# Retention attention ahead of two MLPs: the chunk of 256 tokens worked in two pieces of 128

## The chip, the cores and the metric

One core of one Trainium2 chip runs the whole program in one launch. The metric is the device time of that launch in microseconds (us); lower is better. Of a kernel's runs the median counts.

## The reference

```python
def _attn_ref(q, k, v):                       # (4, 8, 768, 64), float32
    gamma = 1.0 - 2.0 ** (-5.0 - np.arange(H))
    scale = 1.0 / np.sqrt(D)
    for t in range(S):
        state = gamma * state + np.einsum('bhd,bhe->bhde', k[:, :, t], v[:, :, t])
        y[:, :, t] = scale * np.einsum('bhd,bhde->bhe', q[:, :, t], state)

def reference(...):
    x = attn_out.transpose(0, 2, 1, 3).reshape(3072, 512)
    h = x @ w_in;  x = np.maximum(0.01 * h, h) @ w_out          # d_ff 2048
    h = np.maximum(x @ w2_in, 0.0);  return h * h @ w2_out
```

A state of 64x64 per batch and head decays by gamma with each token and takes up one outer product of key and value; each token's output is its query times the state. The result goes through two MLPs.

## The kernel before, in words

The sequence of 768 tokens is cut into NC = 3 chunks of C = 256 tokens, of which each has 4 batches and 4 pairs of heads, so 16 *pairs* per chunk and 48 in all (the list `ups`, lines 120 and 121). Two heads of 64 dimensions share the 128 partitions. Within a chunk the attention is done as matrix products, between chunks a state is carried:

- `load_pair` (line 127) fetches a pair's queries, keys, values and keys again in another layout. In the first chunk a pair is one tile of 512 KB with eight buffers; later a pair has two tiles `r`.
- `prep_pair` (line 142) makes, on VectorE (DVE), `qs` = queries times the decay since the chunk's start (chunks 2 and 3) and `vs` = values times the decay to its end (chunks 1 and 2).
- `scores` (line 159) makes on TensorE (PE) keys times queries for both heads into two PSUM banks `sc`: the second 128 keys against the second 128 queries (128 columns), the first 128 keys against all 256 queries (256 columns). DVE multiplies the three blocks of 128 columns by the mask with the decay into `pm` (line 176).
- `values` (line 180) sums in one PSUM bank `y` (its pool has one buffer) `state` times `qs` (chunks 2 and 3), then the values times `pm`. ScalarE (ACT) copies `y` to `xs` (line 200), the input of the MLP. Then `sp` = keys times `vs`, a matmul of 128x128 in another bank, of which the two diagonal blocks go into the state: by ACT in the first chunk (line 211), by DVE in the second (line 213).

float32 matmuls run as two passes each, so PE's records are twice the matmuls. The matmuls of the two heads use different halves of the array and run side by side.

`mm` (line 111), `load` and `store` pin the order of PE, of SyncE's DMA queue (SP) and of GpSimd's (POOL) to the order of the code. DVE and ACT are ordered by a scheduler as the program is built, and each then runs strictly in that order. `attend` (line 240) does the scores of pair n+1 and then the values of pair n.

The first chunk's 16 pairs run almost alone on PE at the start of the program, two pieces of the first MLP (`emit_plain`) standing among the last pairs. Meanwhile ACT and DVE convert the first weights: `cast` (line 271) takes `sg` as loaded, two operations on ACT (lines 275, 276), three on DVE (277, 278, 281); `pair_up` (line 300) splits the result into two halves, one copy on ACT (301) and one subtraction on DVE (302); `split` (line 56 of that part, 417 and 418 of the file) does the same with `xs`, giving `xh` and `xl`. The pairs of the chunks 2 and 3 are strewn into the first MLP's blocks b = 0 and 1: eight each through `score_next` and `value_to` in the loop over q (lines 826 to 859), eight each through `attend` in the loop over i (line 893).

Of the kernel before, what the change touches and what calls it, by code (L numbers as in the profile page):

```python
# [9 lines left out]
F32 = mybir.dt.float32  # L10
# [4 lines left out]
ALU = mybir.AluOpType  # L15

B, H, S, D = 4, 8, 768, 64
P = 128
C = 256
NC = S // C  # L20
NU = B * NC
NP = H // 2
# [3 lines left out]
T = 512  # L26
# [6 lines left out]
WARM = 10  # L33
# [17 lines left out]
def retention_then_two_mlps(  # L51
# [11 lines left out]
    nc = tc.nc  # L63
# [9 lines left out]
    ps_a = ctx.enter_context(tc.tile_pool(name="ps_a", bufs=1, space=bass.MemoryType.PSUM))  # L73

    early = ExitStack()
    a_p = early.enter_context(tc.tile_pool(name="a", bufs=2))
    const = early.enter_context(tc.tile_pool(name="const", bufs=1))
    late = {}

    def swap_pools():  # L80
        early.close()
        late["p"] = mid.enter_context(tc.tile_pool(name="late", bufs=1))

    def swap_left():
# [7 lines left out]
    qt = const.tile([P, NP, C], F32, name="qt")  # L92
    vt = const.tile([P, NP, 2, 2], F32, name="vt")
    mk = const.tile([P, NP, 2, 384], F32, name="mk")
    gt = const.tile([P, NP], F32, name="gt")
    state = const.tile([P, B, NP, D], F32, name="state")

# [13 lines left out]
    def mm(**kw):  # L111
        pin(nc.tensor.matmul(**kw))  # L112
# [9 lines left out]
    raw, prep, sc_ps = {}, {}, {}  # L122
    xs = {}


# [1 line left out]
    def load_pair(up):  # L127
        u, p = up
        k = u * NP + p
        n = ups.index(up)  # L130
        if u < B:
            t = g_p.tile([P, 2, T], F32, tag=f"t{n % NQ}", name="r", bufs=1)
            load(out=t.rearrange("p i c -> p (i c)"), in_=first[k])
            raw[up] = [t[:, 0], t[:, 1]]
            return
        m = T if u // B < NC - 1 else C
        t = [a_p.tile([P, T], F32, tag=f"r{i}", name="r", bufs=2 + i) for i in range(2)]
        load(out=t[0], in_=first[k, :, 0:T])
        load(out=t[1][:, :m], in_=first[k, :, T:T + m])
        raw[up] = t  # L140

    def prep_pair(up):
        u, p = up
        qk, vk = raw[up]
        qs = vs = None
        if u >= B:
            qs = a_p.tile([P, C], F32, tag="qs", name="qs", bufs=1)
            nc.vector.tensor_tensor(out=qs, in0=qk[:, 0:C], in1=qt[:, p], op=ALU.mult)
        if u < (NC - 1) * B:
            vs = a_p.tile([P, 2, 2, D], F32, tag="vs", name="vs")  # L150
            nc.vector.tensor_tensor(
                out=vs,
                in0=vk[:, 0:C].rearrange("p (b h e) -> p b h e", b=2, h=2),
                in1=vt[:, p].unsqueeze(3).to_broadcast([P, 2, 2, D]),
                op=ALU.mult,
            )
        prep[up] = (qs, vs)

    def scores(up):
        u, p = up  # L160
        qk, vk = raw[up]
        k0 = 2 * (ups.index(up) % 2)
        if u < B:
            sc = [ps_acc.tile([P, 512], F32, tag=f"acc{k0 + h}", name="sc") for h in range(2)]
        else:
            sc = [ps_h.tile([P, 512], F32, tag="h", name="sc") for h in range(2)]
        for cols, kk, qq in ((slice(128, 256), slice(P, 2 * P), slice(P, 2 * P)), (slice(256, 512), slice(0, P), slice(0, C))):
            for h in range(2):
                a = slice(64 * h, 64 * h + 64)
                mm(out=sc[h][:, cols], lhsT=qk[a, C + kk.start:C + kk.stop], rhs=qk[a, qq], start=True, stop=True)  # L170
        pm = []
        if u < B:
            both = x_p.tile([P, 2, T], F32, tag=("xh7", "xl7", "xh2", "xl2")[ups.index(up) % 4], name="pm")
        for h in range(2):
            t = both[:, h, 0:384] if u < B else a_p.tile([P, 384], F32, tag="pm", name="pm")
            nc.vector.tensor_tensor(out=t, in0=sc[h][:, 128:512], in1=mk[:, p, h], op=ALU.mult)  # L176
            pm.append(t)
        sc_ps[up] = pm

    def values(up):  # L180
        u, p = up
        c, b = divmod(u, B)
        vk = raw[up][1]
        qs, vs = prep.pop(up)
        pm = sc_ps.pop(up)
        y = ps_a.tile([P, 2, C], F32, tag="y", name="y")
        if c:
            for h in range(2):
                a = slice(64 * h, 64 * h + 64)
                mm(out=y[a, 0], lhsT=state[a, b, p], rhs=qs[a], start=True, stop=False)  # L190
        for sb in range(2):
            c0, o = (P, 0) if sb else (0, P)
            for h in (1, 0):
                mm(
                    out=y[64 * h:64 * h + 64, 0, c0:C], lhsT=vk[:, sb * P + h * D:sb * P + h * D + D],
                    rhs=pm[h][:, o:o + C - c0], start=sb == 0 and not c, stop=sb == 1,
                )
        if c not in xs:
            xs[c] = x_p.tile([P, KB, TB], F32, tag="xs", name="xs")
        nc.scalar.copy(xs[c][:, p, b * C:b * C + C], y[:, 0])  # L200
        if c < NC - 1:
            sp = ps_h.tile([P, P], F32, tag="h", name="sp")
            for sb in range(2):
                mm(
                    out=sp, lhsT=vk[:, C + sb * P:C + (sb + 1) * P], rhs=vs[:, sb].rearrange("p h e -> p (h e)"),
                    start=sb == 0, stop=sb == 1,
                )
            for h in range(2):
                a = slice(64 * h, 64 * h + 64)
                if c == 0:  # L210
                    nc.scalar.copy(state[a, b, p], sp[a, a])
                else:
                    nc.vector.scalar_tensor_tensor(
                        out=state[a, b, p], in0=state[a, b, p], scalar=gt[a, p:p + 1], in1=sp[a, a],
                        op0=ALU.mult, op1=ALU.add,
                    )
        raw.pop(up)

    n_load, n_prep, n_done = [0], [0], [0]
# [13 lines left out]

    def value_to(n):
        while n_done[0] < n:
            values(ups[n_done[0]])
            n_done[0] += 1
            loads_to(n_done[0] + 2)
# [401 lines left out]
    def second_half(b, q, pa):  # L640
# [5 lines left out]
        pb = ps_a.tile([P, 2, C], F32, tag="y", name="pb").rearrange("p h c -> p (h c)")  # L646
# [107 lines left out]

    zero = o_p.tile([P, T], F32R, tag="gh", name="zero")
    nc.vector.memset(zero.bitcast(F32), 0.0)
    idle = ps_a.tile([P, 2, C], F32, tag="y", name="idle")
    for n in range(WARM):
        nc.tensor.matmul(
            out=idle.rearrange("p h c -> p (h c)"), lhsT=zero[:, 0:P], rhs=zero, start=n == 0, stop=n == WARM - 1  # L760
        )
    nc.scalar.dma_start(out=mk[:, 0], in_=mask[:, 0])
    nc.scalar.dma_start(out=vt, in_=vtab)
    n0 = B * NP
    for p in range(1, NP):
        loads_to(2 * p)
# [10 lines left out]
        elif n in (11, 14):  # L777
            emit_plain(0, (n - 11) // 3, 0)
    split_first(1)
    nc.scalar.dma_start(out=qt, in_=qtab)  # L780
    nc.scalar.dma_start(out=gt, in_=gtab)

    def read_x(b):
        xs[NB + b] = x_p.tile([P, KB, TB], F32, tag="xs", name="xs")
# [133 lines left out]
def _tables():  # L918

    gam = (1.0 - 2.0 ** (-5.0 - np.arange(H, dtype=np.float32))).astype(np.float64)  # L920
    t = np.arange(C)
    qt = gam[:, None] ** t / np.sqrt(D)
    qtab = np.repeat(qt.reshape(NP, 2, 1, C), D, axis=2).reshape(NP, P, C).transpose(1, 0, 2)
    vt = gam[:, None] ** (C - t)
    vtab = vt.reshape(NP, 2, 2, P).transpose(3, 0, 2, 1)
    s, c = np.arange(P)[:, None], np.arange(P)[None, :]
    dec = gam[:, None, None] ** np.maximum(c - s, 0) * (c >= s)
    far = gam[:, None, None] ** (c - s + P)
    mask = np.concatenate([dec, dec, far], axis=2) / np.sqrt(D)
    mask = mask.reshape(NP, 2, P, 384).transpose(2, 0, 1, 3)  # L930
    gtab = np.repeat((gam ** C).reshape(NP, 2, 1), D, axis=2).reshape(NP, P).T
    return [np.ascontiguousarray(a, dtype=np.float32) for a in (qtab, vtab, mask, gtab)]


# [43 lines left out]
```

## Time and profile before

| what | us |
|---|---|
| three runs | 1142.53, 1143.72, 1150.15 |
| median | 1143.72 |
| the profiled execution | 1143.77 |
| its span, first to last instruction | 1141.6 |
| first matmul of the attention to the last of the first chunk | 6.0 to 54.2 |

The trace is of one execution. PE is TensorE's matmuls, PEld its weight loads, which overlap them; DVE, ACT, POOL, SP as above; a q behind a name is its queue of DMA issues. Ends of matmuls are modelled, so rows of one engine may overlap a little and the starts are what is read. Window times count from the span's start.

### The profile page before, as it was taken

To read this page: it belongs to the slowest core of one execution; us is meant where nothing else is said; L and a number is where in the kernel's file an instruction comes from. 1 tells how busy PE (TensorE), PEld (TensorE's weight loads), DVE (VectorE), ACT (ScalarE), POOL (GpSimd) and SP (SyncE) were. 2 spreads that over 40 slices of the span, in tenths; PEclk is the share of its full clock that TensorE was granted. 3 is DMA by queue.
4 is the path that set the end of the run, shared out by engine and by line. 5 is a ranking of instruction groups with operands and counts; after the bars stand their busy time and mean duration, and the time that the engine had idled before them with its cause. 6 is when DMAs were issued, how large, how long until landed. Compare 5 with 4: busy or idle time off the path is not lost.

```text
span 1141.6 us, 14068 instructions
## 1 busy us (share of the span) xinstructions
PE 1121.3 (98%) x5306; PEld 874.8 (77%) x5306; DVE 682.0 (60%) x1018; ACT 546.4 (48%) x863; POOL 74.3 (7%) x130
## 2 busy tenths in 40 slices
PE   8999999999999999999999999999999999999998
PEld 5677777767777776788888887788788888888886
DVE  5866565655443535544457567777457877555853
ACT  3745453323434333344455366665256655455542
POOL 0000000001000000000001011101011100000000
PEclk9999999999999999999999999999999999999999
DMA  9665653655555455479788878957869967257571
GB/s 373 251 236 209 221 221 121 219 178 202 194 198 203 174 190 185 157 276 345 257 320 317 316 275 327 378 212 256 294 225 359 390 211 307 83 192 247 195 241 56
DMA packets 75011, 274.35 MB, mean 240 GB/s; under 512 B 6976, under 2 KB 9024, under 8 KB 64704
## 3 DMA queue, kind: packets, MB, share of 16 engines
q1 hardware_dynamic: 57120, 197.54, 48.6%
q0 software_dynamic: 17248, 74.98, 17.2%
q8 instruction: 42, 0.69, 0.2%
q10 hardware_dynamic: 576, 0.93, 0.2%
q14 instruction: 25, 0.20, 0.1%
HBM read 197.93 MB, written 75.50 MB: 240 GB/s over the span
## 4 chain that ended last, share of the span: by engine, by line
PE 87%; DMA 7%; ACT 3%; DVE 2%; issue 1%; SPq 0%; DVEq 0%; ACTq 0%
PE acc L112 41%; PE pa L112 25%; PE pd L112 8%; PE pb L112 5%; PE y L112 4%; DMA wf<-wraw 4%; PE sc L112 3%; DMA sg<-w 1%; DMA wo<-wou 1%; PE sp L112 1%; DMA r<-first 1%; ACT sg L276 1%; ACT wf L275 0%; ACT wa L301 0%; ACT of L275 0%
## 5 line engine op out<-in xcount | busy, mean ns | idle before, releaser
L112 PE MATMUL acc<-gh,wo 128*128 128x512 f32 x800 | 211.4, 395 | 2.2 <-DMA wo<-wou 2.2
L112 PE MATMUL pa<-xh,wa 128*128 128x512 f32 x576 | 181.3, 396 | 2.3 <-ACT g L462 1.7
L112 PEld LDWEIGHTS acc<-gh,wo 128*128 128x128 f32 x800 | 149.4, 188 | 38.0 <-issue 2.5
L112 PE MATMUL acc<-rot,wu 128*128 128x512 f32 x672 | 157.2, 395 | 0.0
L112 PEld LDWEIGHTS acc<-rot,wu 128*128 128x128 f32 x672 | 126.2, 188 | 30.6
L112 PEld LDWEIGHTS pa<-xh,wa 128*128 128x128 f32 x576 | 106.3, 188 | 28.6 <-ACT g L532 2.6
L112 PE MATMUL acc<-gl,wo 128*128 128x512 f32 x400 | 113.7, 392 | 0.0
L112 PE MATMUL pa<-xl,wa 128*128 128x512 f32 x288 | 113.0, 392 | 0.3 <-DVE xl L418 0.3
L112 PE MATMUL pa<-xh,wb 128*128 128x512 f32 x320 | 101.0, 397 | 0.0
L112 PE MATMUL pd<-xh,wa 128*128 128x512 f32 x320 | 99.3, 391 | 0.9 <-ACT g L462 0.9
L553 DVE TENSOR_TENSOR gl<-g,gh 128x512 fp32r<-128x512 f32 x100 | 67.7, 689 | 52.6 <-PE acc L112 32.2
L112 PEld LDWEIGHTS acc<-gl,wo 128*128 128x128 f32 x400 | 75.2, 188 | 16.6
L112 PE MATMUL acc<-gg,wo 128*128 128x512 f32 x336 | 83.5, 397 | 0.0
L552 ACT CAST gh<-g 128x512 fp32r<-128x512 f32 x100 | 60.5, 619 | 47.4 <-PE acc L112 47.2
L112 PEld LDWEIGHTS acc<-gg,wo 128*128 128x128 f32 x336 | 62.7, 188 | 14.8 <-issue 0.7
L112 PEld LDWEIGHTS pa<-xh,wb 128*128 128x128 f32 x320 | 59.8, 190 | 16.0 <-ACT g L467 2.5
L112 PEld LDWEIGHTS pd<-xh,wa 128*128 128x128 f32 x320 | 59.8, 188 | 15.1 <-ACT g L462 2.5
L618 DVE TENSOR_TENSOR rot<-gu,rot 128x512 fp32r<-128x512 f32 x80 | 54.8, 689 | 26.8 <-ACT rot L617 26.5
L617 ACT CAST rot<-gu 128x512 fp32r<-128x512 f32 x80 | 49.7, 621 | 42.1 <-PE acc L112 36.8
L467 ACT ACTIVATE g<-g 128x512 f32<-128x512 f32 x48 | 30.3, 632 | 82.1 <-DVE g L492 36.9
L176 DVE TENSOR_TENSOR pm<-sc,mk 128x384 f32<-128x384 f32 x96 | 49.2, 551 | 29.4 <-PE sc L112 27.1
L112 PEld LDWEIGHTS pa<-xl,wa 128*128 128x128 f32 x288 | 54.1, 188 | 12.3 <-DVE xl L418 0.7
(112 smaller groups left out, 1581.4 us busy)
## 6 DMA issues: line engine op xcount, KB each, us to landing
wo<-wou SPq DMA_DIRECT2D x40, 1024.0 KB, 7.2
sg<-w SPq DMA_DIRECT2D x32, 1024.0 KB, 9.3
wa<-wid SPq DMA_DIRECT2D x29, 1024.0 KB, 8.0
wu<-wou SPq DMA_DIRECT2D x56, 512.0 KB, 4.8
wb<-wid SPq DMA_DIRECT2D x29, 768.0 KB, 6.9
wou<-wo POOLq DMA_DIRECT2D x16, 1024.0 KB, 5.7
r<-first SPq DMA_DIRECT2D x48, 256.0 KB, 3.5
wid<-wa POOLq DMA_DIRECT2D x11, 1024.0 KB, 4.3
```

The costliest lines, as they stand in the source:

```text
L112: pin(nc.tensor.matmul(**kw))
L176: nc.vector.tensor_tensor(out=t, in0=sc[h][:, 128:512], in1=mk[:, p, h], op=ALU.mult)
L276: nc.scalar.activation(out=lo, in_=lo, func=AF.Copy, scale=2.0 ** -29)
L467: nc.scalar.activation(out=g, in_=g, func=AF.Lrelu)
L552: mark[0] = nc.scalar.copy(gh, g).ins
L553: mark[1] = nc.vector.tensor_tensor(out=gl, in0=g, in1=gh.bitcast(F32), op=ALU.subtract).ins
L617: mark[0] = nc.scalar.copy(r[:, 0], s).ins
L618: mark[1] = nc.vector.tensor_tensor(out=r[:, 1], in0=s, in1=r[:, 0].bitcast(F32), op=ALU.subtract).ins
```

## The change

Each chunk of 256 tokens is worked as two pieces s = 0, 1 of 128. There is no block of first keys against second queries any more: the state is carried from piece to piece. `scores` makes two products of 128 columns; `pm` and the mask shrink from 384 to 256 and from 384 to 128 columns; `qs` and `vs` use one table of 128 for both pieces. `increment` (new) makes keys times `vs` of one piece, two matmuls of 64 columns, one per head, which lie in two halves of the array's columns. `middle` (new) makes `s1`, the state between the pieces: a copy on ACT in the first chunk, a multiply-add on DVE later. `values` now sums in one bank: `state` times `qs` of piece 0 (not in the first chunk), `s1` times `qs` of piece 1, the increment of piece 1, the increment of piece 0 of the *next* pair where that pair's scores are made already (`then`), and the values times `pm`. Behind it stand the copy to `xs` on ACT, the new state on DVE, and `middle` of the next pair, all three reading that bank. Where the next pair isn't made yet (`alone`, in `score_next`), its increment of piece 0 goes into the spare columns of its first bank of scores, behind the scores. The tables `gt` and `qt` are loaded at the start, and the pool of `y` is closed with the attention's others (MLP 2 gets its own, `ps_b`).

```diff
     def prep_pair(up):
...
+        s0 = 1 if u < B else 0
+        qs = a_p.tile([P, 2, P], F32, tag="qs", name="qs", bufs=1)
+        nc.vector.tensor_tensor(
+            out=qs[:, s0:], in0=qk[:, s0 * P:C].rearrange("p (s t) -> p s t", t=P),
+            in1=qt[:, p].unsqueeze(1).to_broadcast([P, 2 - s0, P]), op=ALU.mult,
+        )
...
+    def increment(up, s, sp, start=True):
+        vk, vs = raw[up][1], prep[up][1]
+        for h in range(2):
+            o = C + s * P + h * D
+            mm(
+                out=sp[64 * h:64 * h + 64], lhsT=vk[:, o:o + D], rhs=vs[:, s, h],
+                start=start, stop=True, skip_group_check=True,
+            )
+    def middle(up, sp):
+        u, p = up
+        c, b = divmod(u, B)
+        s1 = mids[up] = a_p.tile([P, D], F32, tag="s1", name="s1", bufs=3)
+        if c == 0:
+            nc.scalar.copy(s1, sp)
+        else:
+            nc.vector.scalar_tensor_tensor(
+                out=s1, in0=state[:, b, p], scalar=gt[:, p:p + 1], in1=sp, op0=ALU.mult, op1=ALU.add,
+            )
     def scores(up):
...
-        for cols, kk, qq in ((slice(128, 256), slice(P, 2 * P), slice(P, 2 * P)), (slice(256, 512), slice(0, P), slice(0, C))):
+        for s in range(2):
+            t = slice(s * P, s * P + P)
...
-    def values(up):
+    def values(up, then=None):
...
+        for s in range(0 if c else 1, 2):
+            st = s1 if s else state[:, b, p]
...
+        if c < NC - 1:
+            increment(up, 1, y[:, C:C + D], False)
+        if then:
+            increment(then, 0, y[:, C + D:C + 2 * D], False)
...
-        nc.scalar.copy(xs[c][:, p, b * C:b * C + C], y[:, 0])
+        nc.scalar.copy(xs[c][:, p, b * C:b * C + C], y[:, 0:C])
...
+            nc.vector.scalar_tensor_tensor(
+                out=state[:, b, p], in0=s1, scalar=gt[:, p:p + 1], in1=y[:, C:C + D], op0=ALU.mult, op1=ALU.add,
+            )
+        if then:
+            middle(then, y[:, C + D:C + 2 * D])
...
-    def score_next(last):
+    def score_next(last, alone=True):
...
-            scores(ups[n])
+            sc = scores(ups[n])
+            if alone or n == n_done[0]:
+                increment(ups[n], 0, sc[:, C:C + D])
+                middle(ups[n], sc[:, C:C + D])
...
     def attend(last):
...
-        score_next(last)
+        score_next(last, False)
```

In the first chunk, ACT's queue from the copy of pair 3 to that of pair 5 stood so before (what a row waits for, in brackets, is the engine whose count it awaits; `xh` is the split of `xs`, `wf` and `sg` the first weight conversion):

```order
L200 COPY xs<-y 128x256 [waits PE_49]
L417 CAST xh_376<-xs 128x1024 [waits Activation_49]
L211 COPY state<-sp 64x64 [waits PE_49]
L211 COPY state<-sp 64x64
L200 COPY xs<-y 128x256 [waits PE_49]
L211 COPY state<-sp 64x64 [waits PE_49]
L211 COPY state<-sp 64x64
L275 ACTIVATE wf<-sg 128x1024 [waits DMAHW7_49]
L276 ACTIVATE sg<-sg 128x1024
L200 COPY xs<-y 128x256 [waits PE_49]
```

and stands so now, over the same stretch (`s_298` and `s_328` are the `s1` of the pairs 4 and 5):

```order
L238 COPY xs<-y 128x256 [waits PE_49]
L451 CAST xh_432<-xs 128x1024 [waits Activation_49]
L178 COPY s_298<-y 128x64 [waits DVE_49]
L309 ACTIVATE wf<-sg 128x1024 [waits DMAHW7_49]
L310 ACTIVATE sg<-sg 128x1024
L238 COPY xs<-y 128x256 [waits PE_49]
L178 COPY s_328<-y 128x64 [waits DVE_49]
L238 COPY xs<-y 128x256 [waits PE_49]
```

The copies that follow `xs` awaited PE before and await DVE now; the two conversions of `sg` stand one pair earlier. On PE, `s_298` and its like are awaited by the next pair's first matmul, here the values of the pairs 1 and 2 and what lies between:

```order
L113 MATMUL y<-qs,s_196 64x128 [waits Activation_49]
L113 MATMUL y<-qs,s_196 64x128
L113 MATMUL y<-vs,r 64x64 x4
L113 MATMUL y<-pm,r 64x128 x4
L113 MATMUL sc<-r 128x128 [waits DMAHW0_49]
L113 MATMUL sc<-r 128x128 x3
L113 MATMUL y<-qs,s_226 64x128 [waits Activation_49]
```

Only the four matmuls `sc<-r` stand between one pair's last matmul and that wait. In the second chunk a pair whose increment is made with its scores stood so on PE before:

```order
L112 MATMUL pa<-xl_604,wa 128x512
L112 MATMUL sc<-r 128x128 [waits DMAHW3_49,Activation_49]
L112 MATMUL sc<-r 128x128 [waits Activation_49]
L112 MATMUL sc<-r 128x256 x2
L112 MATMUL pa<-xh_599,wa 128x512 [waits Activation_49]
```

and now, at the same place:

```order
L113 MATMUL pa<-xl_702,wa 128x512
L113 MATMUL sc<-r 128x128 [waits DMAHW3_49,Activation_49]
L113 MATMUL sc<-r 128x128 [waits Activation_49]
L113 MATMUL sc<-r 128x128 x2
L113 MATMUL sc<-vs,r 64x64 [waits DMAHW4_49,DVE_49]
L113 MATMUL sc<-vs,r 64x64
L113 MATMUL pa<-xh_697,wa 128x512 [waits Activation_49]
```

The increment came in between, and awaits a count of DVE: that of the mask product (line 203) which reads the same bank.

## Rows read from the trace of the kernel before

**Rows 1.** Page, busy time of each engine over the whole span

```profile
PE 1121.3 (98%) x5306; PEld 874.8 (77%) x5306; DVE 682.0 (60%) x1018; ACT 546.4 (48%) x863; POOL 74.3 (7%) x130
```

**Rows 2.** Windows, first chunk, a product in it: length, busy per engine, clock, DMA, GB/s

```profile
6.00:54.24 48.24, 43.05 (x346) 29.55 (x345) 37.33 (x65) 28.03 (x63) 1.39 (x2) 1.00 0.84 331
...
46.75:49.70 2.95, 2.95 (x16) 2.16 (x14) 1.31 (x3) 2.36 (x5) 0.72 (x1) 1.00 0.39 151
```

**Rows 3.** Timeline, PE, one pair of the first chunk: start, length, operation, count

```profile
14.03 0.87 PE L112 MATMUL y<-pm,r 128*64 128x256 f32 x8
14.83 0.71 PE L112 MATMUL sp<-vs,r 128*128 128x128 f32 x4
...
16.32 0.87 PE L112 MATMUL y<-pm,r 128*64 128x256 f32 x8
```

**Rows 4.** Timeline, ACT, the same stretch (idle before it and its releaser in brackets)

```profile
14.94 0.37 ACT L200 COPY xs<-y 128x256 f32<-128x256 f32 x1 [1.24 <-PE y L112]
...
17.64 1.05 ACT L417 CAST xh<-xs 128x1024 fp32r<-128x1024 f32 x1
```

**Rows 5.** Groups by form, 0 to 480 us: busy, mean ns | idle before

```profile
L151 DVE TENSOR_TENSOR vs<-r,vt 128x256 f32<-128x256 f32 x32 | 13.4, 423 | 9.4 <-DMA vt<-vtab 6.0 <-PE sp L112 2.2 <-DMA r<-first 0.8
...
L213 DVE SCALAR_TENSOR_TENSOR state<-state,gt,sp 64x64 f32<-64x64 f32 x32 | 8.8, 276 | 1.3 <-PE sp L112 1.0
...
L211 ACT COPY state<-sp 64x64 f32<-64x64 f32 x32 | 6.6, 206 | 2.5 <-PE sp L112 2.3
```

**Rows 6.** Timeline, the conversion of the first weights on ACT and DVE

```profile
23.03 1.12 ACT L275 ACTIVATE wf<-sg 128x1024 f32<-128x1024 f32 x1 [2.44 <-DMA sg<-w]
...
25.26 1.22 DVE L278 SCALAR_TENSOR_TENSOR wf<-sg,wf 128x1024 uint32<-128x1024 uint32 x1
```

**Rows 7.** Windows, columns as in group 2, while the first chunk's loads run

```profile
18.00:21.00 3.00, 2.99 (x28) 1.82 (x27) 2.58 (x5) 1.79 (x6) 0.00 (x0) 1.00 1.00 408
```

**Rows 8.** Timeline, PE, one pair of the second chunk among the first MLP's matmuls

```profile
75.46 0.93 PE L112 MATMUL sc<-r 64*128 64x128 f32 x8
76.00 0.38 PE L112 MATMUL sc<-r 64*128 64x256 f32 x2
76.32 0.73 PE L112 MATMUL pa<-xh,wa 128*128 128x512 f32 x2
...
82.04 0.65 PE L112 MATMUL y<-qs,state 64*64 64x256 f32 x4
82.62 0.87 PE L112 MATMUL y<-pm,r 128*64 128x256 f32 x8
83.42 0.71 PE L112 MATMUL sp<-vs,r 128*128 128x128 f32 x4
83.89 0.71 PE L112 MATMUL pa<-xh,wa 128*128 128x512 f32 x2
```

**Rows 9.** Groups by form, weight loads of 64 and of 128 columns

```profile
L112 PEld LDWEIGHTS y<-pm,r 128*64 128x64 f32 x384 | 23.6, 136 | 29.4 <-issue 10.6 <-ACT state L211 4.4 <-ACT xs L200 3.0
L112 PEld LDWEIGHTS sp<-vs,r 128*128 128x128 f32 x128 | 16.7, 190 | 5.5 <-issue 5.5
```

**Rows 10.** Timeline, DVE, two mask products of the second chunk's pairs

```profile
59.99 1.02 DVE L176 TENSOR_TENSOR pm<-sc,mk 128x384 f32<-128x384 f32 x2
...
76.42 1.02 DVE L176 TENSOR_TENSOR pm<-sc,mk 128x384 f32<-128x384 f32 x2 [0.25 <-PE sc L112]
```

**Rows 11.** Timeline, PE: first values, what follows the sixteenth, what follows pair 16's scores

```profile
9.14 0.87 PE L112 MATMUL y<-pm,r 128*64 128x256 f32 x8 [0.87 <-DVE pm L176]
...
54.24 0.71 PE L112 MATMUL pa<-xh,wa 128*128 128x512 f32 x2
...
58.62 0.51 PE L112 MATMUL pa<-xh,wa 128*128 128x512 f32 x1
```

**Rows 12.** A wait on PE in the third chunk, and the window behind it (PE, clock, DMA)

```profile
337.88 1.07 PE L112 MATMUL sc<-r 64*128 64x128 f32 x6 [1.56 <-DVE g L488]
...
337.80:343.00 5.20, 5.12 (x18) 0.67 0.84 342
```

More of the change, by code (lines that the diff above doesn't have):

```diff
@@ L72, in retention_then_two_mlps @@
     ps_h = ctx.enter_context(tc.tile_pool(name="ps_h", bufs=3, space=bass.MemoryType.PSUM))
-    ps_a = ctx.enter_context(tc.tile_pool(name="ps_a", bufs=1, space=bass.MemoryType.PSUM))
     early = ExitStack()
+    ps_a = early.enter_context(tc.tile_pool(name="ps_a", bufs=1, space=bass.MemoryType.PSUM))
     a_p = early.enter_context(tc.tile_pool(name="a", bufs=2))
@@ L81, in swap_pools @@
         early.close()
+        late["ps"] = ctx.enter_context(tc.tile_pool(name="ps_b", bufs=1, space=bass.MemoryType.PSUM))
         late["p"] = mid.enter_context(tc.tile_pool(name="late", bufs=1))
@@ L144, in prep_pair @@
         qk, vk = raw[up]
[L145 to L155, printed above, removed]
-            )
-        prep[up] = (qs, vs)
+        s0 = 1 if u < B else 0
[4 more added lines that the diff above has]
+        )
+        n = 2 if u < (NC - 1) * B else 1
+        vs = a_p.tile([P, 2, 2, D], F32, tag="vs", name="vs")
+        nc.vector.tensor_tensor(
+            out=vs[:, 0:n],
+            in0=vk[:, 0:n * P].rearrange("p (s h e) -> p s h e", h=2, e=D),
+            in1=vt[:, p].unsqueeze(1).unsqueeze(3).to_broadcast([P, n, 2, D]),
+            op=ALU.mult,
+        )
+        prep[up] = (qs, vs)
+    def increment(up, s, sp, start=True):
[5 more added lines that the diff above has]
+                start=start, stop=True, skip_group_check=True,
+            )
+    def middle(up, sp):
[8 more added lines that the diff above has]
+            )
     def scores(up):
         u, p = up
-        qk, vk = raw[up]
+        c, b = divmod(u, B)
+        raw_qk = raw[up][0]
         k0 = 2 * (ups.index(up) % 2)
@@ L174, in scores @@
         for h in range(2):
-            t = both[:, h, 0:384] if u < B else a_p.tile([P, 384], F32, tag="pm", name="pm")
-            nc.vector.tensor_tensor(out=t, in0=sc[h][:, 128:512], in1=mk[:, p, h], op=ALU.mult)
+            t = both[:, h, 0:C] if u < B else a_p.tile([P, C], F32, tag="pm", name="pm")
+            nc.vector.tensor_tensor(
+                out=t.rearrange("p (s t) -> p s t", t=P), in0=sc[h][:, 0:C].rearrange("p (s t) -> p s t", t=P),
+                in1=mk[:, p, h].unsqueeze(1).to_broadcast([P, 2, P]), op=ALU.mult,
+            )
             pm.append(t)
         sc_ps[up] = pm
-    def values(up):
+        return sc[0]
+    def values(up, then=None):
         u, p = up
@@ L183, in values @@
         vk = raw[up][1]
[L184 to L187, printed above, removed]
+        qs, vs = prep[up]
+        pm, s1 = sc_ps.pop(up), mids.pop(up)
+        y = ps_a.tile([P, T], F32, tag="y", name="y")
+        for s in range(0 if c else 1, 2):
+            st = s1 if s else state[:, b, p]
             for h in range(2):
                 a = slice(64 * h, 64 * h + 64)
-                mm(out=y[a, 0], lhsT=state[a, b, p], rhs=qs[a], start=True, stop=False)
-        for sb in range(2):
-            c0, o = (P, 0) if sb else (0, P)
+                mm(
+                    out=y[a, s * P:s * P + P], lhsT=st[a], rhs=qs[a, s],
+                    start=s == 0 or not c, stop=False, skip_group_check=True,
+                )
+        if c < NC - 1:
+            increment(up, 1, y[:, C:C + D], False)
+        if then:
+            increment(then, 0, y[:, C + D:C + 2 * D], False)
+        for s in range(2):
             for h in (1, 0):
                 mm(
-                    out=y[64 * h:64 * h + 64, 0, c0:C], lhsT=vk[:, sb * P + h * D:sb * P + h * D + D],
-                    rhs=pm[h][:, o:o + C - c0], start=sb == 0 and not c, stop=sb == 1,
+                    out=y[64 * h:64 * h + 64, s * P:s * P + P], lhsT=vk[:, s * P + h * D:s * P + h * D + D],
+                    rhs=pm[h][:, s * P:s * P + P], start=False, stop=True, skip_group_check=True,
                 )
@@ L199, in values @@
             xs[c] = x_p.tile([P, KB, TB], F32, tag="xs", name="xs")
-        nc.scalar.copy(xs[c][:, p, b * C:b * C + C], y[:, 0])
+        nc.scalar.copy(xs[c][:, p, b * C:b * C + C], y[:, 0:C])
         if c < NC - 1:
[L202 to L216, printed above, removed]
+            nc.vector.scalar_tensor_tensor(
+                out=state[:, b, p], in0=s1, scalar=gt[:, p:p + 1], in1=y[:, C:C + D], op0=ALU.mult, op1=ALU.add,
+            )
+        if then:
+            middle(then, y[:, C + D:C + 2 * D])
+        prep.pop(up)
         raw.pop(up)
@@ L235, in value_to @@
         while n_done[0] < n:
-            values(ups[n_done[0]])
+            up = ups[n_done[0]]
             n_done[0] += 1
+            then = ups[n_done[0]] if n_done[0] < n_prep[0] else None
+            values(up, then if then not in mids else None)
             loads_to(n_done[0] + 2)
@@ L756, in retention_then_two_mlps @@
     nc.vector.memset(zero.bitcast(F32), 0.0)
-    idle = ps_a.tile([P, 2, C], F32, tag="y", name="idle")
+    idle = ps_h.tile([P, T], F32, tag="h", name="idle")
     for n in range(WARM):
         nc.tensor.matmul(
-            out=idle.rearrange("p h c -> p (h c)"), lhsT=zero[:, 0:P], rhs=zero, start=n == 0, stop=n == WARM - 1
+            out=idle, lhsT=zero[:, 0:P], rhs=zero, start=n == 0, stop=n == WARM - 1
         )
@@ L763, in retention_then_two_mlps @@
     nc.scalar.dma_start(out=vt, in_=vtab)
+    nc.scalar.dma_start(out=gt, in_=gtab)
+    nc.scalar.dma_start(out=qt, in_=qtab)
     n0 = B * NP
```

32 lines of the change are left out of this document (14 added, 18 removed).

## The prediction

> **What bounds the kernel now.** I read the page's busy times first: PE is busy for 98% of the span [rows 1]. In windows by stage the first chunk stands out: in 48.24 us PE is busy for 43.05, DVE for 37.33, ACT for 28.03 [rows 2]. On PE's timeline a pair of this chunk has a fixed beat, 14.03 to 16.32 = 2.30 us [rows 3], and PE stands still in it only for single pairs. ACT copies `y` to `xs` beside the next matmuls: it starts .11 after the matmul that follows `y` (14.83, 14.94) [rows 3, 4]. So PE's own work bounds every stage, and ACT and DVE work in its shadow. The question for the change is whether they stay there.
>
> **Shares of the groups on PE.** Scores took 75.46 to 76.32 = .86, the last 256-column pass with the hand-over behind it 76.00 to 76.32 = .32 [rows 8]. With a for a 128-column pass and h for a hand-over, 6a + 2h = .86 and 2a + h = .32, so a is about .107 and h .11. State times `qs` took .58, values times `pm` .80, `sp` .47 (82.04, 82.62, 83.42, 83.89) [rows 8]. With one block of 128 columns in three gone:
> - scores .86 - 2a = .65; values times `pm` .80 - 2a = .59, or .54 behind a group of its own shape (my choice).
> - state times `qs`: .58 stays in the chunks 2 and 3; half of the columns, .37, is new in the first.
> - `sp` (.47) goes; an increment is new: per head two passes of 64 columns, the heads in two halves of the columns, so I count two passes in time. Before shows no such matmul. From below half of a, .055; from above a whole, .11 (cost set by the load of weights and not by columns). I take .08, the middle: .16 an increment, .32 where it stands by itself behind scores (two changes of shape, .08 each).
>
> Loads of 64 columns were 136 ns in the mean against 190 for 128 [rows 9], so they shrank, but not to half. The Trainium skill ("TensorE: Matmul & The Clock Gate", section "LDWEIGHTS (loading the stationary operand)") lets the time of a load go by its columns; by that rule the increment's loads are half as long and the pass costs .055, and the sum below would be some 1149. The ratio here, .72, disagrees with one half.
>
> **The first chunk.** Values now take .37 + .16 + .16 + .54 = 1.23. If nothing waited, a pair were .65 + 1.23 = 1.88 instead of 2.30, 6.7 us less for 16. But the order shows that the three readers of `y` await one another: `xs` on ACT, then the state on DVE, then `s1` of the next pair on ACT, and the next pair's first matmul awaits that. Copies before awaited PE alone. From the end of a pair's values: .11 to the start of `xs` [rows 3, 4], .37 for it [rows 4], .03 hand-over (my estimate, as for the next two), state .28, .03, `s1` .20 (as the copy and the multiply-add of 64x64 in [rows 5]), .06 to PE = 1.08. Only the scores, .65, cover it; .43 shows on PE. The pair is then 1.23 + 1.08 = 2.31, as long as before.
>
> The Trainium skill ("PSUM — Partial Sum Buffer", section "PSUM bank collisions raise a hardware error") says that two engines must not read the same bank and partitions at once, so that readers have to be kept apart by semaphores. That is what the order shows. The bank before had one reader, so no row of before has such a wait; without it the first chunk would gain as in the third rival.
>
> Each conversion that stands in ACT's or DVE's queue between these steps now adds to the chain instead of running beside it. I walked both queues of the changed program pair by pair with the lengths 1.05 (`xh`), 1.12 (each of the two on ACT), 1.22 (on DVE) [rows 4, 6], and took as beginning of a conversion the later of its queue's place and its load. Beyond 1.08 stand: `xh` .67 at pair 4 (1.01 from start to start, less the .34 of the state with its hand-overs, which runs beside it); `wf`, `sg` 1.9 at pair 5; DVE's half of them 1.8 at pair 6; `wa` and the next load's .76 and 2.35 at the pairs 8 and 9; `of`, `wo` 3.1 at pair 10; `xh` .67 at pair 12; .1 later. Together 11.3. Bounds: 5, if each was hidden behind scores and the hand-over to half; 15, if the loads come later than I take. The tables are smaller: 4 masks of 384 KB become 128, `qt` 512 becomes 256, 1.31 MB in all, which at 408 GB/s with DMA full [rows 7] is 3.2 us; so the first conversion comes at some 20 us instead of 23.03 [rows 6]. That moves it to earlier pairs and, as the pairs keep the beat, gives PE nothing.
>
> Sum: 16 values of 1.23 = 19.7; 15 gaps, 13 by the chain 1.08 = 14.0, and 2 that hold a piece of the first MLP with scores, 3.43 each = 6.9 (.65 and 2.95 [rows 2], less .17 of hand-overs that stand in the groups' times already); the last pair has no next increment, -.16; conversions 11.3: 51.7. The start is 9.14 before [rows 11]; smaller `qs` of the first pair makes it 9.05. The end is then about 60.8 instead of 54.24 [rows 11]: **+6.6 us**.
>
> **Between the chunks.** Pair 16 is scored with an increment of its own, which awaits its mask product because both use one bank. Before, that product began at 59.99, 1.37 after its scores' end at 58.62 [rows 10, 11], behind conversions; with .42 for 256 columns (the row of `vs` [rows 5]) and .06, PE waits 1.9 here. The first product awaits `xl` behind one conversion of 1.13 (1.22 with its start) that the longer chain pushes there. **+3.0 us**; from below 0, if DVE's queue has run empty by then.
>
> **The chunks 2 and 3.** Of the 32 pairs 18 make their increment behind their scores. It awaits the mask product of head 0. That began .10 after the scores' end (76.32, 76.42) [rows 8, 10], lasts .42 now, .06 to PE: .58 of wait, with nothing of PE's in it. Behind it on PE's queue stand products of the MLP whose data are there already; all of them come later. The others have theirs beside the values of the pair ahead.
> - Chunk 2, before .86 + .58 + .80 + .47 = 2.71. By itself: .65 + .32 + .58 + .58 + .16 + .54 = 2.83, 8 pairs, +1.0. Beside: .65 + .58 + .16 + .16 + .54 = 2.09, 7 pairs, -4.3.
> - Chunk 3, before .86 + .58 + .80 = 2.24. By itself: .65 + .32 + .58 + .58 + .59 = 2.72, 9 pairs, +4.3. Beside: .65 + .58 + .16 + .54 = 1.93, 7 pairs, -2.2.
>
> Here the chain through `xs`, state and `s1` is covered by MLP products, and nothing else awaits DVE's shorter mask products. **-1.2 us**.
>
> Total +6.6 + 3.0 - 1.2 = +8.4. The profiled execution is 1143.77 (the span 1141.6 and 2.2 around it), the median 1143.72, so nothing has to be shifted: **1152 us**, +.7%.
>
> **Rivals.**
> 1. *The clock falls in the new waits (other side: slower by over 1%).* In the third chunk PE waited 1.56 us and then ran for 337.80 to 343.00 at a mean granted clock of .67, so partly at 1.2 of 2.4 GHz: 5.2 x .33 = 1.7 us lost [rows 12]. For: the change makes waits of 1.9 to 3.1 us in the first chunk and .58 between busy stretches 18 times; against: in the first chunk the clock stayed at 1.00 over its 5 us without work on PE (48.24 - 43.05) [rows 2]. It decides if single waits come to about 1.5 us. With four falls +6.8: 1159, between 1155 and 1163.
> 2. *The covers hold.* Conversions at their lower bound (-6) with the passes at .055 (some -3) bring the first chunk to even: 1138 to 1147, about 1143. For: ACT had 20 us idle in the first chunk (48.24 - 28.03) [rows 2]. Against: these idle times lay after the copies, where the chain now passes.
> 3. *The readers of the bank don't await one another, and DVE is done before the increment.* Then the first chunk gains 5.5 (the 6.7, less some of the conversions) and the later chunks 11: about 1127. The order speaks against it; only a wait long over when it is reached would do this.
>
> **Chances and range.** Forecast, 1147 to 1155: .50. First rival .29, second .18, third .03. One per cent (11.4 us) is about what a measurement of this kernel can tell from no change: 1132.3 and 1155.2. Faster by more: the third rival and a tail of the second, .04. Slower by more: the first rival, and the forecast's upper tail, .32 together. Within: .64. The unknown terms at their bounds, pass .055 or .11 (1149, 1155), conversions 5 or 15 (-6, +4), make 1142 to 1159; with most of the first rival the range is 1142 to 1161.
>
> **What would show it.** Right: in the first chunk PE's waits for values name ACT's `s1` (line 178) behind ACT and DVE work, the beat stays at some 2.3 and the last values end near 61; the increments behind scores show about .6 on PE with DVE's `pm` (line 203) as releaser; pair 16's is the longest. A beat near 1.9 shows the chain wrong, an increment of over .4 without a wait the price of the passes wrong, a granted clock below 1.00 ahead of 60 us the first rival. The forecast falls if the last values end by 55 or after 66, or if the waits in the chunks 2 and 3 don't come to some 10 us.

## The result, and the profile after

| | before | changed |
|---|---|---|
| runs beside each other, median us | 1146.33 (4 runs) | 1162.18 (4 runs, 1158.89 to 1164.54) |
| ratio | 1 | 1.0134, 95% interval 1.0108 to 1.016 |
| span of the profiled execution | 1141.6 | 1157.1 |

The changed kernel is 1.3% slower. The forecast was 1152 (range 1142 to 1161): the sign was right, the size half of what came, and the range ended 1 us too low. Of the 10 us between, 2.6 are the kernel before's own: beside the changed one its median was 1146.33, and the forecast had started from 1143.72. One execution each of runs 4 and 9 below took 1819 and 1859 us; it counts in the medians given there and not in the ratios.

Where the time went is seen from matmuls that both programs have, by their start on PE's timeline. Before:

```profile
67.11 0.63 PE L112 MATMUL acc<-gh,wo 128*128 128x512 f32 x2
...
497.58 0.39 PE L112 MATMUL pd<-xl,wa 128*128 128x512 f32 x1
```

and after, beginning with the first values and with what follows the sixteenth (9.14 and 54.24 in [rows 11]):

```profile
9.65 0.69 PE L113 MATMUL y<-qs,s 64*64 64x128 f32 x4 [0.61 <-ACT s L178]
...
68.51 0.72 PE L113 MATMUL pa<-xh,wa 128*128 128x512 f32 x2
...
87.16 0.63 PE L113 MATMUL acc<-gh,wo 128*128 128x512 f32 x2
...
514.57 0.39 PE L113 MATMUL pd<-xl,wa 128*128 128x512 f32 x1
```

The lag is .5 us at the first values, 14.3 behind the first chunk, 20.05 at the first `acc`, and 17.0 when the attention is long over. So the first chunk lost 14.3, the stretch between the chunks 5.8, and the chunks 2 and 3 won 3.1. (The spans differ by 15.5; the last 1.5 came back in the second MLP, which the change doesn't touch.)

The waits of PE over the whole run (what it waited for: us, times, longest) name two new ones:

```profile
PE y L113 <- ACT s L178: 17.0, 11, 5.6
PE sc L113 <- DVE pm L203: 10.9, 20, 1.4
```

Both are those that the forecast named: values that await `s1` copied by ACT, and increments behind their scores that await the mask product. The windows of the changed kernel add what the forecast's sum did not hold (length, PE busy, clock, DMA share, GB/s):

```profile
9.60:12.00 2.40, 2.35 (x22) 0.50 1.04 410
12.00:16.20 4.20, 4.20 (x38) 0.51 1.06 421
16.20:29.70 13.50, 8.75 (x136) 1.00 0.98 387
29.70:33.00 3.30, 3.30 (x32) 0.50 0.64 220
...
40.40:47.30 6.90, 1.29 (x10) 0.50 0.95 395
47.30:53.40 6.10, 6.08 (x29) 0.50 0.24 92
...
74.50:80.00 5.50, 4.99 (x21) 0.50 0.52 171
```

In four stretches the granted clock was 0.50, that is 1.2 GHz, each time after PE had stood still: after 1.39 and .61 us at the first pair, 2.18 before 28.50, 2.48 before 39.06 (5.62 more followed), .86 and 1.46 at 71.0 and 73.2. Before, the clock was 1.00 in the whole first chunk [rows 2].

The beat of an undisturbed pair, at full clock, shows the chain. PE:

```profile
16.80 0.61 PE L113 MATMUL y<-pm,r 128*64 128x128 f32 x8
17.34 0.71 PE L113 MATMUL sc<-r 64*128 64x128 f32 x8
18.44 0.44 PE L113 MATMUL y<-qs,s 64*64 64x128 f32 x4 [0.39 <-ACT s L178]
18.81 0.45 PE L113 MATMUL y<-vs,r 128*64 128x64 f32 x8
19.09 0.61 PE L113 MATMUL y<-pm,r 128*64 128x128 f32 x8
19.63 0.71 PE L113 MATMUL sc<-r 64*128 64x128 f32 x8
```

ACT, in the same stretch:

```profile
17.46 0.37 ACT L238 COPY xs<-y 128x256 f32<-128x256 f32 x1 [1.40 <-PE y L113]
18.18 0.21 ACT L178 COPY s<-y 128x64 f32<-128x64 f32 x1 [0.35 <-DVE state L240]
```

and DVE:

```profile
17.86 0.28 DVE L240 SCALAR_TENSOR_TENSOR state<-s,gt,y 128x64 f32<-128x64 f32 x1 [0.32 <-ACT xs L238]
```

One can read the three readers of `y` after one another: `xs` at 17.46, the state at 17.86 when `xs` is done, `s1` at 18.18 when the state is done, PE at 18.44: 1.10 us from 17.34, under which stand .71 of scores. The beat is 19.63 - 17.34 = 2.29 us.

The worst wait stands at 41 to 47 us. ACT:

```profile
38.81 0.21 ACT L178 COPY s<-y 128x64 f32<-128x64 f32 x1
43.12 1.12 ACT L309 ACTIVATE wf<-sg 128x1024 f32<-128x1024 f32 x1 [4.11 <-DMA sg<-w]
44.14 1.14 ACT L310 ACTIVATE sg<-sg 128x1024 uint32<-128x1024 uint32 x1
45.16 0.36 ACT L238 COPY xs<-y 128x256 f32<-128x256 f32 x1
46.02 1.15 ACT L310 ACTIVATE sg<-sg 128x1024 uint32<-128x1024 uint32 x1 [0.49 <-DMA sg<-w]
47.05 0.21 ACT L178 COPY s<-y 128x64 f32<-128x64 f32 x1
```

The pair's values were done at 40.46, but in ACT's queue the conversion of the next weights stands ahead of its `xs`, and that conversion awaits its load for 4.11 us. SP's queue tells why the load is late:

```profile
19.75 15.54 SPq L116 DMA_DIRECT2D r<-first  x9
35.39 2.83 SPq L116 DMA_DIRECT2D sg<-w  x2
```

Before, the first of these two loads began 3.4 us earlier, and the conversion of `wf` had another place: behind the `xs` of pair 13 on ACT, where it now stands ahead of that of pair 9.

```profile
32.02 11.30 SPq L115 DMA_DIRECT2D sg<-w  x2
48.80 1.11 ACT L275 ACTIVATE wf<-sg 128x1024 f32<-128x1024 f32 x1
```

The loads stand in SP's queue behind the loads of pairs, which await buffers that finished pairs give back. So slower pairs make the load later, a later load the copy, and a later copy the next pairs. How much of the 4.11 us is the later load and how much the earlier place in ACT's queue was not measured apart; run 6 below takes both away.

### The profile page after: what moved, and what is told of

Same layout as the page of the kernel before. It is cut to its first block, busy times and chain, and to the rows that moved or that the text cites. A ratio compares the mean times of both kernels' runs of the same rounds, so it can differ in the third digit from the quotient of the medians.

```text
span 1157.1 us, 14880 instructions
## 1 busy us (share of the span) xinstructions
PE 1113.4 (96%) x5690; PEld 882.5 (76%) x5690; DVE 681.2 (59%) x1082; ACT 541.8 (47%) x847; POOL 74.3 (6%) x130
## 4 chain that ended last, share of the span: by engine, by line
PE 84%; DMA 7%; DVE 4%; ACT 3%; issue 1%; SPq 0%; ACTq 0%; DVEq 0%
PE acc L113 40%; PE pa L113 25%; PE pd L113 8%; PE pb L113 5%; PE y L113 4%; DMA wf<-wraw 3%; PE sc L113 2%; DMA r<-first 2%; DVE pm L203 1%; DMA sg<-w 1%; ACT sg L310 1%; DMA wo<-wou 1%; ACT wa L335 1%; DMA vt<-vtab 0%; DVE g L522 0%
## 5 line engine op out<-in xcount | busy, mean ns | idle before, releaser
L113 PE MATMUL pa<-xh,wa 128*128 128x512 f32 x576 | 184.5, 401 | 4.4 <-ACT g L496 2.4
L113 PE MATMUL pa<-xl,wb 128*128 128x512 f32 x160 | 62.5, 391 | 0.0
```

## The experiments

All are edits of the changed kernel. Ratios are to the kernel before, run beside each; the changed kernel stands at 1.0134.

**1. Increments of the first chunk in a bank of their own.** `xs` is then the only reader of `y`.

```diff
+        own = c == 0 and then
+        g = ps_h.tile([P, T], F32, tag="h", name="inc")[:, 0:P] if own else y[:, C:C + P]
         if c < NC - 1:
-            increment(up, 1, y[:, C:C + D], False)
+            increment(up, 1, g[:, 0:D], bool(own))
         if then:
-            increment(then, 0, y[:, C + D:C + 2 * D], False)
+            increment(then, 0, g[:, D:P], bool(own))
```

(`middle` of the next pair is then called ahead of the state's update, and the scheduler orders ACT and DVE anew.)

> First chunk only: both increments go to a PSUM bank of their own, so the copy to xs is the only reader of y and the next s1 is copied beside the values; nothing else is changed. Chain theory (the three readers of y in turn put every conversion and every late load on PE's path): the waits of values for s1, 17.0 us in the changed kernel, fall below 4, the first chunk ends at 54 to 57 us instead of 68.5, and the whole takes 1147 to 1151. Clock theory (the loss is the half clock, and it is set off by the two waits of the first pair at 6.7 to 9.6 us, which stay): the half clock from 9.6 to 16.2 and the later falls stay, the first chunk ends after 61, and the time is 1155 or more.

Measured: 1147.66 us, ratio 1.0006 [0.9987, 1.0025]; nearly the whole loss is gone. PE's waits from 6 to 50 us, by what they awaited:

```profile
PE y L113 <- DVE qs L148: 2.9, 4, 1.1
PE y L113 <- ACT xs L240: 1.8, 3, 0.7
PE sc L113 <- DVE pm L203: 1.1, 1, 1.1
PE y L113 <- ACT s L178: 0.6, 1, 0.6
```

The wait for `s1` went from 17.0 to .6 us (the first pair's), and the first chunk ended at 50.24, 4 us earlier than before the change; an undisturbed pair took 1.83 us. The clock still fell once at 10 to 13 us, after the first pair's waits, which stayed, so those waits alone don't make the loss. The chain theory holds, and more than expected. What the run shows is the worth of the readers' turn with all that it brings onto the path, since conversions stand elsewhere in the new order. Behind the chunk ACT's next conversions stood ahead of `xh`, and PE waited 2.46 and 1.38 us there, with the clock at half behind it.

**2. Is it y's single buffer, or the order of its readers?** Every second pair's `y` in another bank, increments still inside `y`. DVE, ACT and PE keep exactly the changed kernel's order.

```diff
-        y = ps_a.tile([P, T], F32, tag="y", name="y")
+        if c == 0 and ups.index(up) % 2:
+            y = ps_h.tile([P, T], F32, tag="h", name="y")
+        else:
+            y = ps_a.tile([P, T], F32, tag="y", name="y")
```

> The changed kernel, but in the first chunk every second pair's y lies in another bank, increments still inside y. If the cost was that y has a single buffer (the next pair's values must wait until all readers have left the bank), this helps like the own bank did: the beat of the undisturbed pairs falls from 2.29 to 1.9 us and the time to 1148 to 1153. If the cost is the readers' turn (s1 of the next pair is read from the same bank after xs and after the state, and the next values need s1), the beat stays at 2.29 and the waits for s1 stay near 17 us: 1159 to 1165.

Measured: 1162.13 us, ratio 1.0158 [1.012, 1.0196]; nothing gained.

```profile
PE y L113 <- ACT s L178: 16.3, 11, 5.6
```

The beat stayed at 2.3 us (15.75 to 18.05). So it is the readers' turn in one bank, with `s1` last, and not the bank being occupied.

The Trainium skill ("PSUM — Partial Sum Buffer", section "PSUM bank collisions raise a hardware error") has two engines kept apart by semaphores on one bank and partitions, also where they read different columns, and lets them go side by side on different banks. The two runs agree: 17.0 us of wait with three readers in one bank, .6 with the increments in another, 16.3 with two banks of which each still has all three.

**3. The increments behind scores, one product later.** In the loops over q of the chunks 2 and 3.

```diff
                     score_next(rest)
                     emit_plain(q, 1, 1)
+                    late_increment()
```

(and the same behind the next part of `emit_in`; `late_increment` does the increment and `middle` that `score_next` did.)

> Chunks 2 and 3 only: of the 16 pairs in the loops over q, the increment and s1 come one product of the MLP later instead of right behind the scores. If the wait for the mask product is a real cost, PE's waits of sc for pm fall from 10.9 us in 20 to some 2.5 in 4, and the time falls by 7 to 9 us, to 1153 to 1155. Rival: PE is held later in its place (a product that awaits the bank of the scores, or values that await s1): less than 3 us of gain.

Measured: 1156.11 us, ratio 1.0079 [1.0057, 1.0101], some .55% or 6 us better; the waits for `pm` fell from 10.9 in 20 to this:

```profile
PE sc L113 <- DVE pm L203: 4.7, 4, 1.7
```

That is a little less than expected. That nothing comes again in another place isn't shown: scores wait 4.6 us in 6 for DVE's `g` here and 2.4 in 5 in the changed kernel's trace, though 4.0 in 6 in run 2's, which has no such edit; and one product waits .8 for `pm`.

**4. The first chunk as before, the chunks 2 and 3 as changed.** 384-column masks, `sp` and its copies for c = 0, `increment` and `middle` for the rest.

```diff
     def values(up, then=None):
         u, p = up
         c, b = divmod(u, B)
+        if c == 0:
+            values_old(up)
+            return
```

> The first chunk is worked as in the kernel before (384-column masks, sp, state by ACT from sp), the chunks 2 and 3 as in the changed one. If the whole loss sits in the first chunk and right behind it: the first chunk ends at 54 to 55 us again, and with the later chunks as in the changed kernel (which win some 4 us against before from 20 us on) the time is 1140 to 1145, below before. Rival (the change also costs in the chunks 2 and 3, since 18 pairs wait .5 us each): 1146 to 1151.

Measured: 1145.08 us, ratio 0.9983 [0.9963, 1.0002]. The loss is the first chunk's and what follows it; alone, the chunks 2 and 3 of the change give no difference that these runs can tell from nothing (the upper end of the first expectation, and near the rival's).

**5. As 4, with the increments of 3.**

> The first chunk as before, and in the chunks 2 and 3 the increments of the loops over q one product later. Against the run with the old first chunk (1145.1) the later increments should take off the 6 us that they took off the changed kernel: 1138 to 1141. Rival (those 6 us were partly the clock, which fell less in that run at 70 to 80 us): 1142 or more.

Measured: 1138.36 us, ratio 0.9942 [0.9923, 0.9962]. Some 5 to 7 us come here too (by the ratios, by the medians), where the granted clock was 1.00 all through. In the trace of run 4 it was 0.92 from 340 to 360 us, which makes some 1.6 us (20 x .08). So the greater part is the wait's, and the rival has a share. This version is faster than both kernels.

**6. The second weight conversion held back** behind the last split of the first chunk.

```diff
+                    elif b == 0 and q == 0:
+                        with tc.issue_after(held[0]), tc.issue_after(held[1]):
+                            get_out(lay, b, q + 1)
```

(and the same around `get_in` of q = 1; `held` are the two operations of `split`.)

> The changed kernel, but the second weight conversion (wf, sg and of, sg of q = 1), which stood among the copies of pairs 9 to 15 on ACT and waited there for its load, is issued only behind the last split of the first chunk. Load theory (a late weight load stands on PE's path because ACT does things in order): the wait of 5.6 us at 41 to 47 us falls below 1, with the half clock behind it gone too, the first chunk ends at 59 to 62 instead of 68.5, and the time is 1152 to 1156. Rival: the conversions are needed that early, so the wait comes again at the products of q = 1 (pa for wa) or at the lrelu behind them: 1159 or more.

Measured: 1152.97 us, ratio 1.0076 [1.0046, 1.0106]: 7 to 9 us less (by the ratios, by the medians), without any change of the chain. The wait of 5.62 us is gone, the longest for `s1` is now the one that was 2.48:

```profile
38.62 0.52 PE L113 MATMUL y<-qs,s 64*64 64x128 f32 x4 [2.82 <-ACT s L178]
...
41.70 0.69 PE L113 MATMUL y<-qs,s 64*64 64x128 f32 x4
```

The next pair's values follow at 41.70 instead of 47.32. So this conversion ahead of the copies was worth far more than its 4.11 us on ACT: its wait, the half clock behind it, and less of a queue ahead of `xh` and `xl`. In the two traces run 6 is 12.1 us ahead at the first `acc` (75.10 against 87.16), of which about 1 is there at pair 4 already (20.31 against 21.37) and isn't the edit's. It is 7.5 ahead at the end; its clock falls twice in the later chunks (0.91 from 280 to 300, 0.89 from 470 to 485).

**7. A short fill in every gap.** Behind each pair's scores of the first chunk one product of 128 columns per head is made a second time.

> First chunk only: behind each pair's scores PE makes one 128-column product per head a second time into banks that nobody reads, .2 us of extra work in a gap of .43. Clock theory: with the gaps half filled the granted clock falls less often, the mean clock of the first chunk goes from 0.81 to above 0.9 and the time falls by 4 to 8 us, to 1154 to 1158. Chain theory: the beat of 2.29 us and the waits behind conversions and loads (2.2, 2.5 and 5.6 us) stay, and the clock falls after those as before: gain under 3 us, or a loss of some 1.

Measured: 1174.31 us, ratio 1.0237 [1.021, 1.0265], outside both expectations. The first fall of the clock was gone:

```profile
9.60:16.20 6.60, 6.14 (x96) 1.00 1.04 414
```

and values of the first three pairs stood at 9.72, 12.01 and 14.31 instead of 9.65, 12.91 and 16.15: so that fall had cost 1.9 us in 6.5. But the scheduler answers the longer scores with another order on ACT and DVE (conversions stood ahead of other copies, waits of 3.4, 4.0 and 6.1 us), and the third chunk's clock fell in four windows of 10 us. As a test of the clock's share in the total the run is worthless.

**8. A fill in the three long waits only.** ACT and DVE keep the changed kernel's order but for some instructions.

```diff
+        for k in range({7: 9, 10: 9, 11: 21}.get(ups.index(up), 0)):
+            for h in range(2):
...
+                mm(out=sc[2 + h][:, 0:P], lhsT=raw_qk[a, C:C + P], rhs=raw_qk[a, 0:P], start=True, stop=True)
```

> The changed kernel, but behind the scores of pairs 7, 10 and 11 PE repeats a product of 128 columns 9, 9 and 21 times into banks that nobody reads: 1.9, 1.9 and 4.5 us of work in the waits of 2.2, 2.5 and 5.6 us that stand there. The waits themselves stay (conversions and the late load are as before). If idle time of PE lowers the clock and the clock then costs time of its own: the granted clock stays at 1.00 from 28 to 53 us, values and products behind the three waits take 1.2 and 3 us instead of 2.1 and 4.9, and the time falls by 3 to 6 us, to 1156 to 1159. If the half clock only hid under the chain: within 1.5 us of the changed kernel (1162). If the repeats come to stand on the path: slower.

Measured: 1165.73 us (1159.6 to 1168.87), ratio 1.0171 [1.0117, 1.0224]: no gain in total. Nor did the clock stay at 1.00 from 28 to 53 us: it was 0.50 from 34.4 to 37.0, behind a wait of 2.21 us in a place that has no fill. Behind the longest wait it does what the clock theory says:

```profile
47.30:53.40 6.10, 5.77 (x60) 1.00 0.23 89
```

and from this pair's values to the next scores it took 47.63 to 51.76 = 4.13 us against 47.32 to 54.31 = 6.99. The lead of 2.6 us at 62 us is still 2.3 at 280 and 1.0 when the attention is over; some 6 us are lost between 800 and 950 us, with loads of the second MLP 3.1 and 1.9 us late, which the edit doesn't touch. That a fall of the clock costs time on the path is shown for its stretch; what all falls make of the total was not settled.

**9. The edits of 1, 3 and 6 together, and 10. with two small ones more** (a second buffer for `qs`; a copy of one column on ACT before the first pair).

> Three edits together on the changed kernel: the first chunk's increments in a bank of their own, the increments of the loops over q one product later, the second weight conversion behind the last split. If the three costs are separate: own bank alone took 14.5 us off, the later increments 6, and the split (waits of 2.5 and 1.4 us with a fall of the clock behind them in the own-bank run) 3 to 5: 1135 to 1140, faster than both kernels. If the conversion held back comes late instead: 1141 to 1147.

> All three edits of the run with 1139.7 us, and two small ones: qs gets a second buffer (values waited 2.6 us in 4 for it there), and ACT makes a copy of one column before the first pair, so that the load of its table doesn't stand before the first s1. If both waits go, 2 to 4 us less: 1136 to 1138. Rival: DVE is as busy as before in the first chunk and the same conversions come late in another place: 1139 to 1141.

Measured: 1139.66 us, ratio 0.9946 [0.9924, 0.9968], and 1136.46 us, ratio 0.9921 [0.9901, 0.9942]. The tenth run is the best: .8% below the kernel before and 2% below the changed one, both intervals clear. Some of what PE still waited for until 50 us in it:

```profile
22.71 0.44 PE L113 MATMUL y<-qs,s 64*64 64x128 f32 x4 [0.48 <-ACT xs L240]
25.59 0.34 PE L113 MATMUL inc<-vs,r 128*64 128x64 f32 x4 [0.35 <-DVE vs L154]
28.12 0.34 PE L113 MATMUL inc<-vs,r 128*64 128x64 f32 x4 [0.48 <-DVE vs L154]
30.29 0.43 PE L113 MATMUL y<-qs,s 64*64 64x128 f32 x4 [0.75 <-ACT xs L240]
```

These are half microseconds: most of the conversions are hidden again, as before the change. The first pair still waits (1.01 and .59 us), with the clock at 0.50 behind it from 11 to 13 us.

## Why the prediction was right and wrong

**The groups on PE: right.** At full clock `qs` .37, two increments .28, values times `pm` .54 (18.44 to 19.63 above), against .37, .32 and .54. Two increments of two passes make .07 a pass, between the forecast's bounds .055 and .11. (Counted out, the forecast's sum holds 154 such passes, 62, 60 and 32 in the three chunks, so these bounds make 1148 and 1157 and not 1149 and 1155.)

**The chain: right.** 1.10 us against 1.08, the beat 2.29 against 2.31, and the experiments 1 and 2 show cause and kind. No row of before has this wait; the order of the changed program alone had it.

**The conversions on the chain: right as a place, mis-sized at one.** The term was 11.3 us with bounds 5 to 15. One step failed in it: "took as beginning of a conversion the later of its queue's place and its load". I walked the queues with loads that come as early as before, or earlier for the smaller tables. I didn't follow that slower pairs hold their buffers longer, that nine loads of pairs wait for these in SP's queue, and that the weights stand behind them. At pair 10 the walk had 3.1 beyond the chain's .43, three conversions without a wait for their load; the wait was 5.62, so 2.1 were missing. That run 6 takes 1153.0, about the 1152 that I forecast, is coincidence: it has no conversion at that place at all, and still three falls of the clock in the first chunk. Luck is also in the sum of the waits: behind the first pair PE waited 16.4 us for `s1` (17.0 less .61), and the sum had 13 gaps of .43 and the 11.3, which make 16.9. But at half clock the longer scores hide the chain, so that the values at 30.85 wait for nothing.

**The clock: the step that failed most.** The sum had no term for it. It stood among the rivals with .29 and four falls of 1.7 us, because before the clock had held at 1.00 over 5 us without work. That spoke of gaps under 1 us but for one; the chain with a conversion in it makes gaps of 1.4 to 5.6. The waits which I had myself put down as 1.8 to 3.1 us were beyond the 1.56 behind which the third chunk's clock had fallen [rows 12]. Yet the one long wait in the first chunk of before was 2.23 us, and the clock stayed at 1.00 behind it:

```profile
25.63 0.87 PE L112 MATMUL y<-pm,r 128*64 128x256 f32 x8 [2.23 <-ACT xs L200]
```

So the length of a single wait doesn't decide it, as the rival had it; what does is not shown here. The four falls came, two of them (9.6 to 16.2 and 40.4 to 53.4) longer than the one of [rows 12]. Their cost on the path differs. The first took 1.9 us (run 7) and the third 2.9 (run 8). The second, at 29.7, took nothing: from pair 6's values to pair 8's it was 28.50 to 34.68 = 6.18 us, and 27.67 to 34.08 = 6.41 in run 8, where the clock was 1.00 there and PE waited 2.21 us for `s1` instead of .94: conversions set the pace. The fourth took about 2.0: the same twelve matmuls behind pair 16's scores needed 76.66 to 81.58 = 4.92 us, and 58.62 to 61.55 = 2.93 before. PE was busy for 44.07 us of the first chunk, more than the 43.05 of before although it does less work.

**The first pair: left out.** I had it begin at 9.05; it began at 9.65. Its increment stands behind its own scores: 1.39 us for `pm`, then .61 for `s1`. Ahead of that copy ACT loads its table, which before it did at 3.00, when nobody waited:

```profile
8.10 1.28 ACT L178 ACT_TABLE_LOAD   x1 [8.10 <-DVE pm L203]
```

The Trainium skill ("ScalarE: Activation LUTs", section "What ACT_TABLE_LOAD costs") gives 1283 ns for this load; the trace agrees. But the load alone isn't what made the pair late. In run 10, where it comes earlier, the first values stand at 9.67 and wait .59 for `qs`, which awaits its table there (9.23) as in the changed kernel:

```profile
9.20 0.29 DVE L148 TENSOR_TENSOR qs<-r,qt 128x128 f32<-128x128 f32 x1 [0.86 <-DMA qt<-qtab]
```

The first fall of the clock came right behind these two waits, with no wait of the chain ahead of it; in run 1, without the chain, it is there too, though shorter.

**Between the chunks: +3.0 forecast, 5.8 measured.** Of the two terms one came: `xl` behind a conversion, 1.46 for 1.1. The other, 1.9 for the increment of pair 16 and "the longest", was .51, since DVE had nothing ahead of that mask product; the longest of these waits was the first pair's 1.39. What the sum didn't have: `xh` waits too (.86, behind another conversion on ACT), and the fourth fall of the clock.

**The chunks 2 and 3: -1.2 forecast, -3.1 measured.** An increment behind its scores waited .51 in most cases in place of .58, and a pair with it lost .1 in the second chunk as forecast (.12). That the stretch came out better is luck: the third chunk's wait of 1.56 us with its fall of the clock [rows 12] did not come in this execution of the changed kernel, which is some 3 us. Without that it would have come out near 0.

In all: the first chunk was missed by 7.7, of which the clock's first and third falls are 4.8, the late load 2.1 and the first pair .6. The stretch between the chunks was missed by 2.8, the later chunks by -1.9, and -1.5 came in the second MLP. Together these are the 15.5 - 8.4 = 7.1 between the spans' difference and the forecast's. The rival of the clock was the better forecast (1159); neither had the late load. The other rivals fell: the covers didn't hold, and the readers do await one another.

## What to carry to other kernels

Before a result is put into the spare columns of a bank, count that bank's readers by engine: if its last reader makes what the next step needs, all readers ahead of it, and whatever stands between them in their queues, come onto the path. Here an own bank for 128 columns was worth 1.3%. Where waits like these (1.4 to 5.6 us) newly appear again and again on a busy matmul engine, put falls of the clock behind them into the sum and not only among the rivals; 2 to 3 us each is what three of four took here, and one was hidden. And where one engine's queue holds both path copies and conversions of loads, ask for each conversion whether it has moved ahead of copies, and for each load what its own queue waits for: a slower consumer makes it later.

## What the runs showed of the hardware that was not expected

- Waits of 2.0 us in two pieces (1.39 and .61, with scores between them) at the first pair came before the clock's fall to 0.50 from 9.6 to 16.2 us, with PE busy for 6.55 of these 6.6 us. With a short fill behind the scores it stayed at 1.00 in the same stretch (run 7), though both waits stayed in part (1.07 and .38 there). A wait of 2.23 us in the kernel before had no fall behind it.
- A fill of useless matmuls changed the total by +12 us in one run and by nothing certain in the other, since the order of the other engines and the later loads move with it: a clock experiment is read in its own stretch, not in the total.
